# A bank table of eight rows for the attention groups in which VectorE raises two scores

## Chip, cores and metric

The kernel runs on one core of one Trainium2 chip. The metric is the device time of one execution in microseconds (us). TensorE is called PE, VectorE DVE, ScalarE ACT and GpSimd POOL, as the profile calls them.

## The reference

One token matrix x of 2048 rows and 512 columns goes through two branches, and a gate per row mixes them:

```
x = A_x
g = _sigmoid((x * gate_w).sum(-1, keepdims=True))
a = _A_ref(x, A_wqkv, A_wo)        # softmax attention: 32 heads of 16, no mask, then wo
b = _B_ref(x, B_w1, B_b1, B_w2, B_b2)   # layer norm, MLP over the token axis, gelu
return g * a + (1 - g) * b
```

In the attention, `scores = q k^T / 4`, `p = softmax(scores)` and `o = p v`, all in fp32.

## The kernel before, in words

The kernel first projects q, k and v, then runs the first layer of the MLP. After that comes the attention stage, which fills the last three quarters of the time and into which the MLP's second layer and the output projection are woven. Only this stage is touched.

**Groups and phases.** There are 32 groups; a group is a pair of heads and one half (1024) of the query columns. A group has eight phases. In each phase PE computes eight score tiles of 128 keys by 512 queries (line 922). Each is a *unit*, numbered 0 to 7 in the order of its score within the phase. A score uses 64 rows of PE's array, and a matmul of the woven-in work (line 1045) runs on the other 64 rows beside most of them, six or eight per phase. Then PE applies the exponentials of the *phase before* to v (`apply_v`, line 878), called *the AV block* here: two instructions per unit, each of them two passes, so 32 passes for eight units, into one bank that holds the sums of the block. DVE adds that bank to the group's running sum (line 898), in one piece or two.

**Who takes the exponentials.** ACT does, in five instructions per phase: two units alone, then three pairs of units whose banks are neighbours (line 945). In 21 of the groups, `EXTRA` (0 to 10 and 15 to 24), the two units of one pair in phase 2 (`EXTRA_PH`) go to DVE instead: `steps_of_exp` reads both banks out (line 985, here called *the two raises*), and nine further DVE instructions per unit, spread over the phases behind, compute the power of two. The raises are issued behind the last score of the phase. To level the AV blocks, a pair of phase 1 is held back from the block of phase 2 and goes into that of phase 3, and the raised pair joins the block after phase 7. The blocks in phases 1 to 7 so have 32, 24, 32, 32, 32, 32 and 32 passes, and the one in phase 0 has 40 when it follows a group of `EXTRA`.

**Banks.** Of the eight PSUM banks, seven are a ring for scores and AV sums (`RING`, the tile `s`), and one holds the woven-in work (`dn`). Which bank each score of a phase gets, which units ACT takes together and in which order, and which bank the AV block writes, is a row of the table `TURN`, used in turn by phase number modulo 3. A score waits until the last reader of its bank has finished: the exponential of the unit that was there, or DVE's addition if it held AV sums. The AV block waits likewise for the reader of its own bank. In all three rows of `TURN` that bank held unit 1 of the same phase, which ACT reads as its second exponential.

**Order.** The stage is written under a manual schedule: every engine executes its instructions in the order of the program text, and the waits between engines come from the recorded reads and writes (`reads`, `writes`). DVE's other work (`slow`, the split of weights, the nine steps) is dealt out phase by phase, ahead of the phase's scores in the text. At a phase's end the text has the raises (in phase 2 of the 21 groups), the AV block and DVE's addition.

Of the kernel before, what the change touches and what calls it, by code (L numbers as in the profile page):

```python
# [76 lines left out]
def gated_mix(ctx: ExitStack, tc: tile.TileContext, a_x, a_wqkv, a_wo, b_w1, b_b1, b_w2, b_b2, gate_w, out):  # L77
# [28 lines left out]
    g = const.tile([P, NS], F32, name="g")  # L106
# [23 lines left out]
    order = {f0: [(c + (NS // 2 if f0 + NB >= F else 0)) % NS for c in range(NS)] for f0 in range(0, F, NB)}  # L130
# [58 lines left out]
    with tc.tile_pool(name="vp", bufs=1, side="right") as pool:  # L189
# [165 lines left out]
        e = pool.tile([P, NS], F32, name="e")  # L355
# [115 lines left out]
    with tc.tile_pool(name="ln1", bufs=3, side="right") as ln, tc.tile_pool(name="gl", bufs=2, side="right") as gl:  # L471
# [21 lines left out]
        beside = {mybir.EngineType.Activation, mybir.EngineType.DVE, mybir.EngineType.Pool}  # L493
# [6 lines left out]
        for f0, cs in order.items():  # L500
            n = min(NB, F - f0) // P
# [68 lines left out]
    for step in gelus:  # L570
# [10 lines left out]


    TURN = [
# [3 lines left out]
    ]  # L587
# [157 lines left out]
    N_S = 8  # L745
# [34 lines left out]
    done, at = at, put_outputs(range(NH), 6, 12, at)  # L780
    at = put_outputs(range(NH, NS), 0, EARLY, at)
# [41 lines left out]
    EXTRA = *range(0, 11), *range(15, 25)  # L823
    EXTRA_PH = 2
# [38 lines left out]
    def apply_v(late, bank):  # L863

        if not late:
            return
        g, units = late
        pairs = list(zip(*([u for u in units if u[2] == qb] for qb in range(2))))
        assert 2 * len(pairs) == len(units)
        av = banks[:, bank, :]  # L870
        taken = [0, 0]

        for pair in pairs:
            for i, c, qb, pt, act in pair:
                taken[qb] += 1
                for h in range(2):
                    j = 2 * qb + h
                    mm = nc.tensor.matmul(  # L878
                        av[32 * j : 32 * j + VC, i * QC : (i + 1) * QC],
                        v[:, c, g % NP * 2 + i, :],  # L880
                        pt[:, h * QC : (h + 1) * QC],
                        start=taken[qb] == 1,
                        stop=taken[qb] == len(pairs),
                    )
                    writes(mm, bank, j, act)

        there = {(i, qb) for i, _, qb, *_ in units}
        if len(there) == 4:
            parts = [(sums[g], av)]
        else:  # L890
            parts = []
            for i in sorted(range(2), key=lambda i: -sum(k[0] == i for k in there)):
                qbs = [qb for qb in range(2) if (i, qb) in there]
                if qbs:
                    at = slice(64 * qbs[0], 64 * (qbs[-1] + 1)), slice(i * QC, (i + 1) * QC)
                    parts.append((sums[g][at], av[at]))
        for x, y in parts:
            reads(nc.vector.tensor_tensor(x, y, x, ALU.add), bank)  # L898

    engines = {getattr(mybir.EngineType, name) for name in ("PE", "Activation", "DVE", "Pool", "SP")}  # L900
    with tc.manual_schedule(engines=engines):
        kt, qt = {0: k_bufs[0]}, {0: q_bufs[0]}
        late, fence = None, None
# [8 lines left out]
                next(step)  # L912
        full(first)

        pt = None

        def score(grp, i, n, turn, exps, units, apart):
# [4 lines left out]
            mm = nc.tensor.matmul(  # L922
                banks[:, bank, :],
                kt[grp][rows, c * P : (c + 1) * P],
                qt[grp][rows, qb * NB : (qb + 1) * NB],
                start=True,
                stop=True,
            )
            writes(mm, bank)
            units.append([i, c, qb, None, None])  # L930
            for which in exps:
                if which[-1] == len(units) - 1:
                    if which == apart:
                        steps_of_exp(turn, units, which)
                    else:
                        exponential(turn, units, which)

        def exponential(turn, units, which):
            nonlocal pt
            if which[0] != 1:  # L940
                pt = ptp.tile([P, 2, NB], F32, name="pt")
            which = sorted(which, key=lambda m: turn[m])
            first, at = which == [1], [turn[m] for m in which]
            dst = pt[:, first : first + len(at), :]
            act = nc.scalar.activation(dst, banks[:, at[0] : at[-1] + 1, :], AF.Exp, scale=SCALE)  # L945
            reads(act, *at)
            for n, m in enumerate(which):
                units[m][3:] = dst[:, n, :], act

        def steps_of_exp(turn, units, which):  # L950

# [36 lines left out]
                reads(ins, turn[m])  # L988
                exp_steps.extend(steps(n, units[m]))

        def without(units, which):
            return [units[m] for m in which], [u for m, u in enumerate(units) if m not in which]

        exp_steps, held, apart = [], [], []
        for grp in range(NG):
            at = [0, 0]
            for ph in range(2 * TWOS):
# [7 lines left out]
                two, second = divmod(ph, 2)  # L1005
# [5 lines left out]
                if not second:  # L1011
                    for what, *args in calls.get(two, ()):
                        what(*args)
                    beside = [step(*args) for step, *args in dense.get(two, ())]
# [16 lines left out]
                    room -= cost  # L1031
                    step()
                units = []
                turn, exps, av_bank = TURN[(2 * two + second) % len(TURN)]

                qbs = [0, 1, 0, 1, 0, 1, *((1, 0) if len(beside) == 6 else (0, 1))]
                pair = [e for e in exps if len(e) == 2 and qbs[e[0]] != qbs[e[1]]][-1]
                alone = pair if grp in EXTRA and ph == EXTRA_PH else None
                half = slice(0, HALF) if second else slice(HALF, P)
                for m, (ps, a, b, first, last, done) in enumerate(beside):  # L1040
                    score(grp, second, at[second], turn, exps, units, alone)
                    if grp == ph == 0 and m < 4:
                        next(gelus[m % 2])
                    at[second] += 1
                    mm = nc.tensor.matmul(ps, a[half], b[half], start=first and not second, stop=last and bool(second))  # L1045
                    if m == 0 and fence is not None:
                        tc.add_manual_dep(mm.ins, fence.ins.name, SYNC, reason=REASON)
                    if m == len(beside) - 1:
                        fence = nc.gpsimd.memset(token, 0.0)  # L1049
                        tc.add_manual_dep(fence.ins, mm.ins.name, SYNC, reason=REASON)  # L1050
                    if done and second:
                        done()
                for n in range(N_S - len(beside)):
                    i = (n + second + 1) % 2
                    score(grp, i, at[i], turn, exps, units, alone)
                    at[i] += 1
                if splits:
                    split_weight(nc.vector.tensor_copy)
# [15 lines left out]
                late = grp, units  # L1074
        assert not slow and not soon and not exp_steps


# [12 lines left out]
            nc.scalar.copy(hi[i], whole[i])  # L1090

        divided(0)
        apply_v(late, TURN[(2 * two + second + 1) % len(TURN)][-1])
# [138 lines left out]
```

## Time and profile before

| | |
|---|---|
| median of 3 runs | 1271.02 us (1270.91 to 1281.69) |
| the profiled execution | 1272.05 us; from its first to its last instruction 1270.3 us |
| granted PE clock in it | 0.998 |
| PE busy, its weight loads | 99%, 63% of the span |
| ACT, DVE, POOL busy | 84%, 57%, 18% |
| exponentials on ACT (line 945) | 1259 instructions, 943.6 us |
| scores, AV passes | 2048 and 8024 + 168 |
| first score, last AV pass | 295.8 us, 1252.8 us from the span's start |

Matmuls are pipelined and drawn longer than the distance between them, so PE reads as busy nearly always. Its waits show in the start times of its instructions and as idle time of its weight loads (PEld), which wait in its place. ACT's instructions are drawn long too when one queues behind another.

### The profile page before, as it was taken

The numbers are of one execution on the slowest core, as the hardware profiler recorded it, in microseconds if no ns is written. First come the engines' busy times: TensorE is split into PE (matmuls) and PEld (weight loads), VectorE is DVE, ScalarE is ACT, GpSimd is POOL, SyncE is SP. The second block draws the span as 40 slices with busy tenths as digits, with TensorE's granted clock in tenths as the row PEclk, the third lists the DMA queues.
The fourth block names the chain that finished last, engine by engine and source line by source line (L and its number), as shares of the span: only waits on it lengthen the run. The fifth ranks groups of instructions, "written<-read, shape, count | busy, mean of one in ns | idle before, by whom it ended". The sixth has DMA issues, their size and how long they took to land.

```text
span 1270.3 us, 33073 instructions
## 1 busy us (share of the span) xinstructions
PE 1262.1 (99%) x13230; PEld 796.6 (63%) x13230; DVE 721.5 (57%) x1326; ACT 1072.3 (84%) x1484; POOL 228.7 (18%) x447
## 2 busy tenths in 40 slices
PE   9999999999999999999999999999999999999998
PEld 7888888886555555555555555555555555555555
DVE  6775361536776776666634346676666662325425
ACT  4444343438999999999999999999999999999994
POOL 4510244553111111111110011111111111100000
PEclk9999999999999999999999999999999999999999
DMA  6787644326343443334555533333433345547621
GB/s 189 217 294 296 225 134 130 95 75 134 72 93 60 77 86 69 77 66 82 121 102 132 117 64 71 68 73 76 74 75 70 76 87 105 99 87 204 142 62 70
DMA packets 101826, 141.19 MB, mean 111 GB/s; under 512 B 17161, under 2 KB 62495, under 8 KB 98528
## 3 DMA queue, kind: packets, MB, share of 16 engines
q1 hardware_dynamic: 101232, 138.20, 46.2%
q8 instruction: 106, 1.74, 0.7%
q10 hardware_dynamic: 432, 0.79, 0.2%
q14 instruction: 56, 0.46, 0.1%
HBM read 102.77 MB, written 36.16 MB: 109 GB/s over the span
## 4 chain that ended last, share of the span: by engine, by line
PE 98%; DMA 0%; DVE 0%; ACT 0%; SPq 0%; issue 0%; ACTq 0%
PE s L878 38%; PE s L922 35%; PE acc L469 12%; PE acc L91 10%; PE dn L1045 2%; PE pa L1116 1%; DMA x<-in_A_x_dram 0%; PE acc L299 0%; PE pa L1125 0%; PE dn L908 0%; PE acc L210 0%; DVE ot L482 0%; SPq L202 0%; DVE base L1144 0%; DVE row L482 0%; ACT row L484 0%
## 5 line engine op out<-in xcount | busy, mean ns | idle before, releaser
L945 ACT ACTIVATE pt<-s 128x512 f32<-128x512 f32 (+1 forms) x1259 | 943.6, 962 | 10.3 <-PE s L922 4.4
L922 PE MATMUL s<-qs,ks 64*128 64x512 f32 x2048 | 493.9, 404 | 0.1
L878 PE MATMUL s<-pt,v 128*17 128x256 f32 x8024 | 482.6, 381 | 0.0
L922 PEld LDWEIGHTS s<-qs,ks 64*128 64x128 f32 x2048 | 325.4, 184 | 170.3 <-ACT pt L945 90.9
L898 DVE TENSOR_TENSOR ot<-s,ot 128x256 f32<-128x256 f32 (+2 forms) x427 | 190.5, 448 | 352.9 <-PE s L878 275.9
L878 PEld LDWEIGHTS s<-pt,v 128*17 128x17 f32 x8024 | 210.3, 97 | 231.9 <-ACT pt L945 82.9
L1045 PE MATMUL dn<-u_hi,w_hi 64*128 64x512 f32 x428 | 186.4, 436 | 0.0
L84 POOL TENSOR_TENSOR w_lo<-w_raw,w_hi 128x512 fp32r<-128x512 f32 (+1 forms) x127 | 150.7, 1189 | 167.9 <-ACT w_hi L83 105.1
L1045 PE MATMUL dn<-u_lo,w_hi 64*128 64x512 f32 x430 | 170.0, 395 | 0.0
L1045 PE MATMUL dn<-u_hi,w_lo 64*128 64x512 f32 x430 | 169.1, 393 | 0.0
L1049 POOL MEMSET token<- 1x1 f32 x256 | 26.2, 102 | 782.6 <-PE dn L1045 704.4
L967 DVE SCALAR_TENSOR_TENSOR row<-row,o_hi 128x512 f32<-128x512 f32 x168 | 116.6, 694 | 4.9
L83 ACT CAST w_hi<-w_raw 128x512 fp32r<-128x512 f32 (+1 forms) x67 | 37.8, 568 | 76.6 <-PE acc L469 57.1
L469 PE MATMUL acc<-h_hi,w_lo 128*128 128x512 f32 x224 | 87.2, 389 | 0.0
L469 PE MATMUL acc<-h_hi,w_hi 128*128 128x512 f32 x224 | 87.1, 389 | 0.0
L469 PE MATMUL acc<-h_lo,w_hi 128*128 128x512 f32 x224 | 87.1, 389 | 0.0
L1045 PEld LDWEIGHTS dn<-u_hi,w_lo 64*128 64x128 f32 x430 | 79.3, 184 | 0.9
L1045 PEld LDWEIGHTS dn<-u_lo,w_hi 64*128 64x128 f32 x430 | 79.4, 185 | 0.3
L1045 PEld LDWEIGHTS dn<-u_hi,w_hi 64*128 64x128 f32 x428 | 78.6, 184 | 0.7
L91 PE MATMUL acc<-xt_hi,wc_hi 128*128 128x512 f32 x128 | 49.8, 389 | 0.0
L91 PE MATMUL acc<-xt_lo,wc_hi 128*128 128x512 f32 x128 | 49.8, 389 | 0.0
L91 PE MATMUL acc<-xt_hi,wc_lo 128*128 128x512 f32 x128 | 49.8, 389 | 0.0
(160 smaller groups left out, 1156.6 us busy)
## 6 DMA issues: line engine op xcount, KB each, us to landing
w_raw<-in_B_w_dram SPq DMA_DIRECT2D x96, 256.0 KB
ks<-kp SPq DMA_DIRECT2D x192, 128.0 KB
qs<-qp SPq DMA_DIRECT2D x256, 64.0 KB
qp<-pc SPq DMA_DIRECT2D x16, 768.0 KB
x<-in_A_x_dram SPq DMA_DIRECT2D x32, 256.0 KB
kp<-pc SPq DMA_DIRECT2D x16, 512.0 KB
w_raw<-in_B_w_dram SPq DMA_DIRECT2D x32, 128.0 KB
bp<-row SPq DMA_DIRECT2D x16, 256.0 KB
```

The source lines that it names most:

```text
L83: copy(hi, src)
L84: return sub(lo, src, hi.bitcast(F32), ALU.subtract)
L91: nc.tensor.matmul(ps, a, b, start=start and n == 0, stop=stop and n == last)
L469: nc.tensor.matmul(p, a, b, start=first and k == 0, stop=last and k == 2)
L878: mm = nc.tensor.matmul(av[32 * j : 32 * j + VC, i * QC : (i + 1) * QC], v[:, c, g % NP * 2 + i, :], pt[:, h * QC : (h + 1) * QC], start=t ...
L898: reads(nc.vector.tensor_tensor(x, y, x, ALU.add), bank)
L922: mm = nc.tensor.matmul(banks[:, bank, :], kt[grp][rows, c * P : (c + 1) * P], qt[grp][rows, qb * NB : (qb + 1) * NB], start=True, stop=True,)
L945: act = nc.scalar.activation(dst, banks[:, at[0] : at[-1] + 1, :], AF.Exp, scale=SCALE)
L967: nc.vector.scalar_tensor_tensor(box[1], q or box[1], a, x, ALU.add, ALU.mult)
L1045: mm = nc.tensor.matmul(ps, a[half], b[half], start=first and not second, stop=last and bool(second))
L1049: fence = nc.gpsimd.memset(token, 0.0)
L1116: nc.tensor.matmul(pa[t], a, b, start=i == 0 and t not in LATE, stop=i == len(mms) - 1 and t in LATE)
```

## The change

A second table, `LEAN`, is used in the 21 groups of `EXTRA`: eight rows, one for each phase of a group. `TURN` goes on serving the other eleven groups. Each row of either table gets a fourth entry that says in which order the AV block later takes the units: `None` keeps the order of the scores, `True` takes pairs of neighbouring scores in the order in which their exponentials end, and `False` pairs them anew in the order of the exponentials. The raised units are no longer the last fitting pair of the row but units 1 and 7 (`APART`) of phase 2, taken out of that row's exponentials. Exponentials now leave a queue in the row's order, each when its last score has been issued. The AV pairs are matched when a phase ends (`matched`), and held or set aside as pairs; the number of passes per block stays.

```diff
     TURN = [
-        ((3, 4, 5, 6, 0, 1, 2, 3), ((0,), (1,), (2, 3), (4, 5), (6, 7)), 4),
+        ((3, 4, 5, 6, 0, 1, 2, 3), ((0,), (1,), (2, 3), (4, 5), (6, 7)), 4, None),
...
+    LEAN = [
+        ((4, 1, 0, 3, 6, 5, 2, 4), ((0,), (2,), (5, 4), (1, 6), (3, 7)), 0, False),
...
+        ((1, 4, 0, 3, 6, 5, 2, 1), ((0,), (7, 2), (4,), (5, 1), (3, 6)), 4, True),
...
+        ((3, 1, 2, 4, 0, 5, 3, 6), ((0,), (2,), (4, 1), (7, 5), (3, 6)), 2, True),
...
+        ((3, 2, 1, 4, 0, 6, 5, 3), ((0,), (1,), (4, 2), (3, 7), (6, 5)), 2, False),
+    ]
+    APART = (1, 7)
...
             units.append([i, c, qb, None, None])
-            for which in exps:
-                if which[-1] == len(units) - 1:
-                    if which == apart:
-                        steps_of_exp(turn, units, which)
-                    else:
-                        exponential(turn, units, which)
+            if apart and len(units) - 1 == apart[-1]:
+                steps_of_exp(turn, units, apart)
+            while queue and max(queue[0]) < len(units):
+                exponential(turn, units, queue.pop(0))
...
-                turn, exps, av_bank = TURN[(2 * two + second) % len(TURN)]
-
-                qbs = [0, 1, 0, 1, 0, 1, *((1, 0) if len(beside) == 6 else (0, 1))]
-                pair = [e for e in exps if len(e) == 2 and qbs[e[0]] != qbs[e[1]]][-1]
-                alone = pair if grp in EXTRA and ph == EXTRA_PH else None
+                table = LEAN[ph] if grp in EXTRA else TURN[(2 * two + second) % len(TURN)]
+                turn, exps, av_bank, by_end = table
+                apart = APART if grp in EXTRA and ph == EXTRA_PH else ()
+                exps = [e for e in ([m for m in e if m not in apart] for e in exps) if e]
+                queue, spare = list(exps), None
...
+                assert not queue
+                pairs = matched(units, exps, False if apart else by_end)
                 if grp in EXTRA:
 
                     if ph == EXTRA_PH - 1:
-                        held, units = without(units, pair)
+                        held = [pairs.pop()]
                     elif ph == EXTRA_PH:
-                        apart, units = without(units, pair)
-                        units = held + units
+                        away = [tuple(sorted((units[m] for m in apart), key=lambda u: u[2]))]
+                        pairs = held + pairs
                     elif ph == 2 * TWOS - 1:
-                        units = units + apart
-                late = grp, units
+                        pairs = pairs + away
+                late = grp, pairs
```

The rows of `LEAN` shown are those of phases 0, 2, 5 and 7. The first bracket of a row has the banks of the eight scores, the second the exponentials, the number behind them is the AV block's bank. The rows of phases 1, 3, 4 and 6 begin `(6, 5, 2, 4, ...)`, `(6, 0, 2, 1, ...)`, `(1, 0, 4, 3, ...)` and `(5, 0, 6, 1, 2, ...)`; their AV banks are 2, 2, 0 and 0.

**How instructions move: PE, phase 2 of the fifth group of `EXTRA`.** `s` is the ring, `qs` and `ks` are the stacked q and k, `dn` is the woven-in work; behind a row stands the engine whose semaphore it waits for. The rows from the last beside-matmul to the AV block, before:

```order
L1045 MATMUL dn<-u_hi,w_lo 128x512
L922 MATMUL s<-qs_2748,ks_2750 128x512 [waits DVE_49]
L922 MATMUL s<-qs_2748,ks_2750 128x512 [waits Activation_49]
L878 MATMUL s<-pt,v 17x256 [waits Activation_49]
L878 MATMUL s<-pt,v 17x256 x11
```

and now:

```order
L1064 MATMUL dn<-u_hi,w_lo 128x512
L932 MATMUL s<-qs_2748,ks_2750 128x512 [waits DVE_49]
L932 MATMUL s<-qs_2748,ks_2750 128x512 [waits Activation_49]
L888 MATMUL s<-pt,v 17x256 [waits DVE_49]
L888 MATMUL s<-pt,v 17x256 x11
```

The AV block's first instruction waits for DVE in place of ACT: its bank 4 now held unit 1, and DVE reads that. It is so in all 21 groups, and was in none before.

**DVE, the same phase, as it stands now** (the third group; before, the rows are the same with lines 898 and 985, and the last has no wait):

```order
L84 TENSOR_TENSOR wo_lo<-o_sum,wo_hi 128x512 [waits DVE_49]
L1007 TENSOR_SCALAR o_hi<-s 128x512 [waits PE_49]
L1007 TENSOR_SCALAR o_hi<-s 128x512 [waits Activation_49]
L908 TENSOR_TENSOR ot<-s,ot 128x256 [waits PE_49,Activation_49]
L908 TENSOR_TENSOR ot<-s,ot 64x256 [waits Activation_49]
```

The two raises stay where they were. The first has a wait for PE, the second has none for PE; in two groups (the second and third) a weight split of two instructions stands right ahead of them, in the other 19 DVE's addition does.

**PE, phase 5 of the fifth group.** Before, scores 2 to 6 and what they wait for:

```order
L922 MATMUL s<-qs_2748,ks_2750 128x512 [waits Activation_49]
L1045 MATMUL dn<-u_hi,w_lo 128x512
L922 MATMUL s<-qs_2748,ks_2750 128x512
L1045 MATMUL dn<-u_hi,w_hi 128x512
L922 MATMUL s<-qs_2748,ks_2750 128x512 [waits Activation_49]
L1045 MATMUL dn<-u_lo,w_hi 128x512
L922 MATMUL s<-qs_2748,ks_2750 128x512
L1045 MATMUL dn<-u_hi,w_lo 128x512
L922 MATMUL s<-qs_2748,ks_2750 128x512 [waits DVE_49]
```

The same scores now:

```order
L932 MATMUL s<-qs_2748,ks_2750 128x512
L1064 MATMUL dn<-u_hi,w_lo 128x512
L932 MATMUL s<-qs_2748,ks_2750 128x512
L1064 MATMUL dn<-u_hi,w_hi 128x512
L932 MATMUL s<-qs_2748,ks_2750 128x512 [waits DVE_49]
L1064 MATMUL dn<-u_lo,w_hi 128x512
L932 MATMUL s<-qs_2748,ks_2750 128x512 [waits Activation_49]
L1064 MATMUL dn<-u_hi,w_lo 128x512
L932 MATMUL s<-qs_2748,ks_2750 128x512 [waits Activation_49]
```

The bank of the last AV block, which DVE's addition must free, is written again by score 4 and no longer by score 6. So it is in phases 5, 6 and 7; in phases 3 and 4 it is score 5, in phases 0 to 2 score 6 as before.

More of the change, by code (lines that the diff above doesn't have):

```diff
@@ L866, in apply_v @@
             return
-        g, units = late
-        pairs = list(zip(*([u for u in units if u[2] == qb] for qb in range(2))))
-        assert 2 * len(pairs) == len(units)
+        g, pairs = late
+        assert all([u[2] for u in pair] == [0, 1] for pair in pairs)
         av = banks[:, bank, :]
@@ L885, in apply_v @@
                     writes(mm, bank, j, act)
-        there = {(i, qb) for i, _, qb, *_ in units}
+        there = {(i, qb) for pair in pairs for i, _, qb, *_ in pair}
         if len(there) == 4:
@@ L913, in gated_mix, with score @@
         full(first)
-        pt = None
-        def score(grp, i, n, turn, exps, units, apart):
+        spare = None
+        def score(grp, i, n, turn, queue, units, apart):
             c, qb = n // 2, (n + i) % 2
@@ L948, in exponential, with matched @@
                 units[m][3:] = dst[:, n, :], act
+        def matched(units, exps, by_end):
+            order = [m for e in exps for m in e]
+            if by_end is False:
+                return list(zip(*([units[m] for m in order if units[m][2] == qb] for qb in range(2))))
+            pairs = [sorted((m, m + 1), key=lambda m: units[m][2]) for m in range(0, N_S, 2)]
+            if by_end:
+                pairs.sort(key=lambda pair: max(order.index(m) for m in pair))
+            return [tuple(units[m] for m in pair) for pair in pairs]
         def steps_of_exp(turn, units, which):
@@ L989, in steps_of_exp @@
                 exp_steps.extend(steps(n, units[m]))
-        def without(units, which):
-            return [units[m] for m in which], [u for m, u in enumerate(units) if m not in which]
-        exp_steps, held, apart = [], [], []
+        exp_steps, held, away = [], [], []
         for grp in range(NG):
@@ L1033, in gated_mix @@
                 units = []
-                turn, exps, av_bank = TURN[(2 * two + second) % len(TURN)]
-                qbs = [0, 1, 0, 1, 0, 1, *((1, 0) if len(beside) == 6 else (0, 1))]
-                pair = [e for e in exps if len(e) == 2 and qbs[e[0]] != qbs[e[1]]][-1]
-                alone = pair if grp in EXTRA and ph == EXTRA_PH else None
+                table = LEAN[ph] if grp in EXTRA else TURN[(2 * two + second) % len(TURN)]
[3 more added lines that the diff above has]
+                queue, spare = list(exps), None
                 half = slice(0, HALF) if second else slice(HALF, P)
                 for m, (ps, a, b, first, last, done) in enumerate(beside):
-                    score(grp, second, at[second], turn, exps, units, alone)
+                    score(grp, second, at[second], turn, queue, units, apart)
                     if grp == ph == 0 and m < 4:
@@ L1054, in gated_mix @@
                     i = (n + second + 1) % 2
-                    score(grp, i, at[i], turn, exps, units, alone)
+                    score(grp, i, at[i], turn, queue, units, apart)
                     at[i] += 1
@@ L1092, in gated_mix @@
         divided(0)
-        apply_v(late, TURN[(2 * two + second + 1) % len(TURN)][-1])
+        apply_v(late, TURN[(2 * two + second + 1) % len(TURN)][2])
         divided(1)
```

15 lines of the change are left out of this document (10 added, 5 removed), and 8 rows, old and new, of tables (LEAN, TURN).

## Prediction

> **What bounds the kernel now.** I read the page first, its chain of waits above all, then the attention stage phase by phase.
>
> ```profile
> PE 98%; DMA 0%; DVE 0%; ACT 0%; SPq 0%; issue 0%; ACTq 0%
> ...
> L922 PEld LDWEIGHTS s<-qs,ks 64*128 64x128 f32 x2048 | 325.4, 184 | 170.3 <-ACT pt L945 90.9
> ...
> L878 PEld LDWEIGHTS s<-pt,v 128*17 128x17 f32 x8024 | 210.3, 97 | 231.9 <-ACT pt L945 82.9
> ```
>
> The chain is PE's nearly throughout, so a wait put into PE's queue moves the end. PE's own waits in the stage are put down to ACT. How much of that is real shows in the phases of group 18, one of the 21, cut at the first score of each (phase 0 to 7):
>
> ```profile
> 831.17:835.33 4.16, 4.16 (x58) 2.38 (x55) 2.68 (x5) 4.16 (x6) 1.84 (x3) 1.00 0.61 170
> 835.33:838.99 3.66, 3.66 (x50) 2.08 (x47) 1.03 (x2) 3.54 (x6) 1.38 (x2) 1.00 0.50 130
> 838.99:842.23 3.24, 3.24 (x42) 1.84 (x39) 2.13 (x4) 3.24 (x5) 0.09 (x1) 1.00 0.74 135
> 842.23:845.90 3.66, 3.66 (x50) 2.10 (x47) 2.84 (x6) 3.40 (x6) 0.09 (x1) 1.00 0.99 113
> 845.90:849.57 3.67, 3.67 (x50) 2.08 (x47) 3.02 (x5) 3.67 (x6) 0.09 (x1) 1.00 0.47 64
> 849.57:853.25 3.68, 3.68 (x50) 2.12 (x47) 2.87 (x6) 3.68 (x6) 0.48 (x2) 1.00 0.01 2
> 853.25:856.96 3.71, 3.71 (x50) 2.14 (x47) 2.93 (x5) 3.71 (x6) 0.43 (x2) 1.00 0.03 7
> 856.96:860.68 3.73, 3.73 (x50) 2.14 (x47) 3.27 (x6) 3.73 (x6) 0.62 (x2) 1.00 0.15 35
> ```
>
> Behind the window stands its length in us. An undisturbed phase with a block of 32 passes takes 3.66. The block of phase 2 has 24 passes and saves 0.42, so phase 0, with 40, would take some 4.08 undisturbed. Phases 5, 6, 7 and 0 are longer than that by 0.02, 0.05, 0.07 and 0.08: that is all that waiting costs here, 0.22 us a group. Its cause is seen in a group whose exponentials are all ACT's:
>
> ```profile
> 720.35:724.08 3.73, 3.73 (x50) 2.14 (x47) 0.85 (x2) 3.73 (x6) 0.09 (x1) 1.00 0.99 146
> ```
>
> There ACT sets the pace at 3.73. In a group of the 21 it falls 0.07 behind in each 3.66 phase after the relief of phase 2, until the AV block, whose bank ACT's second exponential reads, waits for it. If all of this went, 21 x 0.22 = 4.6 us would be won, 0.4% of the time: the ceiling of any gain here.
>
> **The wait added in phase 2.** The AV block's bank there is now unit 1's, and its reader is the first raise on DVE. What that means is in the same phase of group 18, PE first, then DVE:
>
> ```profile
> 838.99 0.50 PE L922 MATMUL s<-qs,ks 64*128 64x512 f32 x1
> ...
> 839.33 0.39 PE L922 MATMUL s<-qs,ks 64*128 64x512 f32 x1
> ...
> 840.49 0.40 PE L922 MATMUL s<-qs,ks 64*128 64x512 f32 x2
> 840.81 1.49 PE L878 MATMUL s<-pt,v 128*17 128x256 f32 x24
> 842.23 0.50 PE L922 MATMUL s<-qs,ks 64*128 64x512 f32 x1
> ```
>
> ```profile
> 839.28 0.88 DVE L898 TENSOR_TENSOR ot<-s,ot 128x256 f32<-128x256 f32 x2 [2.72 <-DMA o<-ot]
> 840.96 1.29 DVE L985 TENSOR_SCALAR o_hi<-s 128x512 f32<-128x512 f32 x2 [0.79 <-PE s L922]
> ```
>
> ```profile
> L985 DVE TENSOR_SCALAR o_hi<-s x42: 679/686/693, 307.0 to 1019.0; 128x512 f32<-128x512 f32 x42
> ...
>   PE s L922: 15.0, 19
> ```
>
> DVE has added by 840.16 and idles 0.79 for PE. This group uses the third row of `TURN`, so the raised units are 3 and 7; unit 3 was scored three scores before the last, and still the first raise begins 0.47 behind the last two scores (840.49). In the order of the program the first raise has a wait for PE and the second has none for PE: one wait, on the last score, serves both. Nothing of that is changed, so with units 1 and 7 the first raise begins at 840.96 again and takes 0.69. What PE needs to notice it is seen where a late addition held up a score:
>
> ```profile
> 1016.92 0.88 DVE L898 TENSOR_TENSOR ot<-s,ot 128x256 f32<-128x256 f32 x2 [3.43 <-DMA s<-ot]
> ...
> 1017.86 0.19 PEld L922 LDWEIGHTS s<-qs,ks 64*128 64x128 f32 x2 [0.35 <-DVE ot L898]
> ```
>
> The addition ends at 1017.80, the score's weight load starts at 1017.86: 0.06. So the block starts at 840.96 + 0.69 + 0.06 = 841.71 where it started at 840.81, **0.90 us later**. Behind it in PE's queue stands the next phase; nothing of PE's can run meanwhile. Times 21: **18.9 us**. In two groups a weight split stands ahead of the raises on DVE:
>
> ```profile
> 336.20 0.69 DVE L84 TENSOR_TENSOR wo_lo<-o_sum,wo_hi 128x512 fp32r<-128x512 f32 x1
> 336.92 1.29 DVE L985 TENSOR_SCALAR o_hi<-s 128x512 f32<-128x512 f32 x2
> ```
>
> ```profile
> 336.42 1.49 PE L878 MATMUL s<-pt,v 128*17 128x256 f32 x24
> ```
>
> There the block starts at 336.92 + 0.75 = 337.67 where it was 336.42, 1.25 later: 2 x 0.35 = **0.7 us** more. So far that cost nothing, since the block's bank was ACT's. Phase 2 also has four exponentials alone and one pair, one instruction more on ACT; even a whole exponential of 0.60 lies inside PE's new pause of 0.9:
>
> ```profile
> 842.77 0.60 ACT L945 ACTIVATE pt<-s 128x512 f32<-128x512 f32 x1 [0.26 <-PE s L922]
> ```
>
> **The addition that must be done sooner.** In phases 5 to 7 score 4 takes the bank that DVE's addition frees. Phase 5 of group 18, DVE and PE:
>
> ```profile
> 849.78 0.88 DVE L898 TENSOR_TENSOR ot<-s,ot 128x256 f32<-128x256 f32 x2 [0.59 <-PE s L878]
> ```
>
> ```profile
> 849.57 0.50 PE L922 MATMUL s<-qs,ks 64*128 64x512 f32 x1
> ...
> 850.61 0.39 PE L922 MATMUL s<-qs,ks 64*128 64x512 f32 x1
> ```
>
> The addition ends at 850.66, noticed at 850.72; score 4 stood at 850.61. It loses 0.11, and the phase takes 3.77: +0.09 in phase 5, +0.04 in phase 7. In phase 6 the addition's two pieces follow each other closer (no wait between them in the program's order) and are just in time. If phase 6 loses 0.11 too, that is 2.3 us more in all. Before, the bank was due two scores later, and nothing waited for it.
>
> **What goes.** With 0.90 us more in phase 2 and 0.11 in phases 5 and 7 ACT catches up, and its lag no longer reaches the AV block: -0.08 in phase 0, -0.05 in phase 6. Per group beside the 0.90: 0.09 + 0.04 - 0.08 - 0.05 = 0.00. The two halves cancel.
>
> **Where the tables meet** (groups 10 to 11, 14 to 15, 24 to 25) one table's early scores fall on banks that the other frees late. The last pair of a phase and the next phase's first score:
>
> ```profile
> 860.26 1.27 ACT L945 ACTIVATE pt<-s 128x1024 f32<-128x1024 f32 x1
> ```
>
> ```profile
> 860.68 0.50 PE L922 MATMUL s<-qs,ks 64*128 64x512 f32 x1
> ```
>
> The pair ends at 861.53, 0.85 into the phase, noticed at 0.91. Group 11's first score wants bank 5, read by the last pair of group 10: +0.9 at most, 0.8 with ACT less late. Group 15's second score, due 0.34 into the phase (839.33 against 838.99), wants bank 1, read by the last pair: +0.5. Group 25's second score wants bank 2, the AV bank, free at 1.09 + 0.06: +0.8. Together **2.1 us**, once.
>
> **Sum:** 18.9 + 0.7 + 0.0 + 2.1 = 21.7 us. The profiled execution took 1272.05 (span 1270.3 and 1.75 around it), so it would take 1293.8; against the median of 1271.02 it is **1292.7 us**, 1.7% slower.
>
> **Rivals.**
>
> *The first raise is not late.* Place: its wait for PE. If it ended with unit 1's score (the second of the phase), DVE would be free at 840.16, begin 0.03 later (as from 336.89 to 336.92 above), the raise be done at 840.88, the block at 840.94: 0.13 instead of 0.90. The point from which it decides: a first raise that starts before 840.06 costs nothing. Then 21 x 0.13 + 2 x 1.1 (the weight split still stands ahead) + 2.1 = 7 us: 1278, 0.6% more and not to be told from no change. For it speaks only that unit 1 is scored early; against it the 0.79 of idling with unit 3 and the single wait. 5%, since what decides it is in the trace.
>
> *The block waits for both raises.* Then it starts at 840.96 + 1.29 + 0.06 = 842.31, 1.50 later: 21 x 1.50 + 2.8 = 34 us, 1305. For it: both raises write one tile. Against it: the second raise reads unit 7's bank, which is not the block's. 3%.
>
> *The clock falls.* PE now stands still for 0.8 us 21 times, more than in any window above, all of which were granted 1.00. If each pause cost one phase at half the clock, 3.66 more, it would be 21 x 3.66 = 77 on top: 1370. No window shows a fall, and the pause is a quarter of a phase: 2%. The Trainium skill bears on this (TensorE: Matmul & The Clock Gate, "A second HAM failure mode: psum-queue depth-cycling"): frequent short idling between groups of matmuls can make the clock swing between half and full. The same page ("What's actually happening") puts the fall behind an idle window of about 3.4 us, which the pause does not fill. The windows above, all at 1.00, hold no pause that long, so no run has shown it yet.
>
> **How the numbers follow.** The forecast has 90%. Its own spread: the raise differs by 0.01, the noticing by perhaps 0.05, the cancelling halves by 0.15 a group, that is 21 x 0.2 = 4 us either way, and the meetings by up to 1. So 1287 to 1298 holds it, and with it more than 8 in 10; the rivals lie outside. A measurement of this kernel can tell 1% from no change, 12.7 us: the forecast, the double wait and the clock are slower by more (95% less 2% for a forecast missed far), the early raise is within it (5% and 1%), and a gain above 1% exceeds the 4.6 us ceiling (1%).
>
> **What would show it.** Right: phase 2 of the 21 groups at 4.1 us, its AV block released by the raise on DVE with about 0.9 us of PE idling; phases 5 and 7 at 3.77 with score 4 released by the addition; phases 0 and 6 at 4.08 and 3.66; the other eleven groups as before but for the three meetings. Wrong: a first raise that starts before the last score; a phase 2 near 3.3; a clock under 0.99; phases 3 to 7 that sum to more than 18.6.

## The result and the profile after

| | before | changed |
|---|---|---|
| time, median | 1271.03 us (6 runs) | 1302.92 us (6 runs, 1302.51 to 1303.61) |
| ratio | | 1.0239, 95% interval 1.021 to 1.0268 |
| span of the profiled execution | 1270.3 us | 1300.8 us |
| mean granted clock | 0.998 | 0.999 |

The medians differ by 31.9 us, 2.5%, inside the interval of the ratio; one of the six runs of the kernel before took 1281.69 us, the others 1270.6 to 1271.93. The forecast was 21.7 us, and the measured time lies above the stated range. In the page of the changed kernel, first the chain of waits, then two rows of the groups (busy time and mean, then the idle time ahead of them):

```profile
PE 90%; ACT 5%; issue 2%; DVE 2%; DMA 0%; SPq 0%; ACTq 0%; DVEq 0%
...
L888 PE MATMUL s<-pt,v 128*17 128x256 f32 x8024 | 482.6, 381 | 17.9 <-DVE o_hi L1007 17.9
L932 PEld LDWEIGHTS s<-qs,ks 64*128 64x128 f32 x2048 | 315.2, 184 | 187.3 <-ACT pt L958 102.2
```

The chain is no longer PE's alone, and the AV matmuls have got an idle time of 17.9 us whose releaser is the raise. That one row gives the size of the wait in phase 2, and it leaves 14 of the 31.9 us unexplained. Group 18 again, cut at the first score of its phases; phases 0, 2, 5, 6 and 7:

```profile
851.82:855.91 4.09, 4.09 (x58) 2.31 (x55) 2.58 (x5) 4.04 (x6) 2.05 (x3) 1.00 0.76 172
...
859.58:863.68 4.10, 3.30 (x42) 1.85 (x39) 2.14 (x4) 3.58 (x6) 0.09 (x1) 1.00 0.83 136
...
871.04:874.93 3.89, 3.89 (x50) 2.00 (x47) 2.87 (x6) 3.88 (x6) 0.91 (x2) 1.00 0.00 0
874.93:879.17 4.24, 3.93 (x50) 2.01 (x47) 2.93 (x5) 3.83 (x6) 0.21 (x2) 1.00 0.02 6
879.17:883.06 3.89, 3.89 (x50) 2.00 (x46) 3.40 (x6) 3.83 (x6) 0.62 (x2) 1.00 0.12 32
```

Phase 2 has grown from 3.24 to 4.10, and PE is busy for only 3.30 of it. Phases 5 and 7 have grown from 3.68 and 3.73 to 3.89, though PE counts as busy throughout: what is lost there does not show as idle time. Phase 6 of this group is longer than in the others (in the median group it takes 3.87), because its addition starts 0.58 into the phase in place of 0.21; why it does in this one group was not found. The clock was 1.00 in all of them.

The next table sums, over the 21 groups, the changed kernel's phases less those of the kernel before, in us; a phase runs from its first score to the next phase's first. The experiments told below stand in it in the same way, and the last column sums the stage from its first score to the start of its last phase:

| kernel | ph 0 | 1 | 2 | 3 | 4 | 5 | 6 | 7 | other groups | all |
|---|---|---|---|---|---|---|---|---|---|---|
| the change | -0.5 | 0.5 | 18.7 | -0.2 | 0.1 | 4.5 | 3.9 | 4.1 | 0.9 | 31.9 |
| early raise | -0.4 | 0.6 | 4.2 | -0.2 | 0.1 | 4.9 | 3.5 | 4.1 | 1.0 | 17.7 |
| units 5 and 7 | -0.6 | 0.4 | -0.7 | 0.1 | 0.1 | 4.5 | 3.9 | 4.1 | 0.9 | 12.7 |
| one piece | 0.6 | 0.4 | 18.8 | -0.2 | 0.0 | 0.0 | 0.0 | 0.8 | 1.0 | 21.4 |
| score 3 | -0.5 | 0.5 | 18.7 | -0.2 | 0.1 | 9.5 | 8.8 | 8.7 | 1.1 | 46.6 |
| units 5 and 7, one piece | 0.6 | 0.6 | -0.6 | 0.0 | 0.1 | 0.1 | -0.1 | 0.7 | 0.9 | 2.3 |
| units 5 and 7, score 5 | 0.9 | 0.4 | -0.7 | 0.0 | 0.0 | 1.5 | 1.3 | 1.3 | 0.9 | 5.8 |
| same partitions | -0.5 | 0.7 | 18.7 | -0.2 | 0.0 | 4.5 | 1.5 | 4.1 | 1.0 | 29.7 |

The loss sits in two places: phase 2, which was forecast, and phases 5 to 7, where 1.7 us were forecast and 12.4 came (0.75 of that is the first meeting of the tables, in phase 7 of group 10). The 31.9 of the last column equals the difference of the medians; the two profiled spans differ by 30.5, since in that execution of the changed kernel the stretches ahead of the first score and from the last phase on were together 1.3 shorter.

**Phase 2** of group 18, PE's rows and then DVE's, with the idle time ahead of a row and its releaser in brackets:

```profile
860.84 0.61 PE L932 MATMUL s<-qs,ks 64*128 64x512 f32 x3
862.26 1.49 PE L888 MATMUL s<-pt,v 128*17 128x256 f32 x24 [0.81 <-DVE o_hi L1007]
863.68 0.50 PE L932 MATMUL s<-qs,ks 64*128 64x512 f32 x1
```

```profile
859.87 0.88 DVE L908 TENSOR_TENSOR ot<-s,ot 128x256 f32<-128x256 f32 x2 [2.72 <-ACT pt L958]
861.51 1.29 DVE L1007 TENSOR_SCALAR o_hi<-s 128x512 f32<-128x512 f32 x2 [0.77 <-PE s L932]
```

DVE idles 0.77 until the last score, the first raise runs from 861.51 to 862.20, and the AV block follows at 862.26. The second raise is still running then (to 862.80): the block waits for the first alone.

**Phase 5** of group 18: PE, PE's weight loads, DVE.

```profile
871.38 0.39 PE L932 MATMUL s<-qs,ks 64*128 64x512 f32 x1
...
871.61 0.39 PE L932 MATMUL s<-qs,ks 64*128 64x512 f32 x1
...
871.84 0.39 PE L932 MATMUL s<-qs,ks 64*128 64x512 f32 x1
...
872.18 0.49 PE L932 MATMUL s<-qs,ks 64*128 64x512 f32 x1
...
872.52 0.39 PE L932 MATMUL s<-qs,ks 64*128 64x512 f32 x1
...
872.75 0.40 PE L932 MATMUL s<-qs,ks 64*128 64x512 f32 x2
```

```profile
871.38 0.18 PEld L932 LDWEIGHTS s<-qs,ks 64*128 64x128 f32 x1
...
871.62 0.18 PEld L932 LDWEIGHTS s<-qs,ks 64*128 64x128 f32 x1
...
872.18 0.18 PEld L932 LDWEIGHTS s<-qs,ks 64*128 64x128 f32 x1 [0.38 <-DVE ot L908]
...
872.29 0.19 PEld L932 LDWEIGHTS s<-qs,ks 64*128 64x128 f32 x1
```

```profile
871.25 0.88 DVE L908 TENSOR_TENSOR ot<-s,ot 128x256 f32<-128x256 f32 x2 [0.61 <-PE s L888]
```

And score 5 in the same phase of the kernel before, which starts at 849.57:

```profile
850.84 0.39 PE L922 MATMUL s<-qs,ks 64*128 64x512 f32 x1
```

In an undisturbed stretch the weight load of a score runs one step, 0.23, ahead of its own matmul: the loads at 871.38 and 871.62 belong to the matmuls at 871.61 and 871.84. The Trainium skill has it so (TensorE: Matmul & The Clock Gate, "Step-by-step: what each phase is for"): weight loads are pulled ahead of the matmuls in flight. These rows agree. Score 4's load would have started at 871.84, but it carries the wait for the addition (done at 872.13) and starts at 872.18, 0.34 late. Its matmul starts with it instead of behind it, is drawn 0.49 long in place of 0.39, and the next score follows 0.34 later (872.52) in place of 0.23. So score 5 stands 1.48 into the phase, where it stood at 1.27: the phase loses 0.21 and not 0.11. PE counts as busy throughout because its matmuls are drawn 0.39 to 0.49 long, longer than even the step of 0.34.

**Phase 6**, in group 5 since group 18's is unusual (it starts at 475.11): DVE, then PE.

```profile
475.32 0.86 DVE L908 TENSOR_TENSOR ot<-s,ot 128x256 f32<-128x256 f32 x2 [0.64 <-PE s L888]
```

```profile
475.92 0.39 PE L932 MATMUL s<-qs,ks 64*128 64x512 f32 x1
...
476.24 0.50 PE L932 MATMUL s<-qs,ks 64*128 64x512 f32 x1
...
476.58 0.39 PE L932 MATMUL s<-qs,ks 64*128 64x512 f32 x1
```

The two pieces take 0.86 together, against 0.88 with a wait between them: having no wait in the order has won 0.02. Score 4 is held here as well, to 1.13 into the phase.

### The profile page after: what moved, and what is told of

Its sections match the earlier page's. It is cut to its first block, busy times and chain, and to the rows that moved or that the text cites. A ratio compares the mean times of both kernels' runs of the same rounds, so it can differ in the third digit from the quotient of the medians.

```text
span 1300.8 us, 33107 instructions
## 1 busy us (share of the span) xinstructions
PE 1273.3 (98%) x13230; PEld 786.5 (60%) x13230; DVE 728.1 (56%) x1333; ACT 1082.8 (83%) x1505; POOL 230.3 (18%) x447
## 4 chain that ended last, share of the span: by engine, by line
PE 90%; ACT 5%; issue 2%; DVE 2%; DMA 0%; SPq 0%; ACTq 0%; DVEq 0%
PE s L888 33%; PE s L932 32%; PE acc L469 12%; PE acc L91 10%; ACT pt L958 5%; PE dn L1064 2%; DVE o_hi L1007 1%; PE pa L1137 1%; PE acc L299 0%; DMA x<-in_A_x_dram 0%; DVE ot L908 0%; PE pa L1146 0%; PE dn L918 0%; PE acc L210 0%; DVE ot L482 0%
## 5 line engine op out<-in xcount | busy, mean ns | idle before, releaser
L958 ACT ACTIVATE pt<-s 128x1024 f32<-128x1024 f32 (+1 forms) x1280 | 953.8, 893 | 31.8 <-PE s L932 25.6
L932 PE MATMUL s<-qs,ks 64*128 64x512 f32 x2048 | 506.7, 407 | 2.2 <-ACT pt L958 1.1
L888 PE MATMUL s<-pt,v 128*17 128x256 f32 x8024 | 482.6, 381 | 17.9 <-DVE o_hi L1007 17.9
L932 PEld LDWEIGHTS s<-qs,ks 64*128 64x128 f32 x2048 | 315.2, 184 | 187.3 <-ACT pt L958 102.2
L908 DVE TENSOR_TENSOR ot<-s,ot 128x256 f32<-128x256 f32 (+1 forms) x434 | 196.0, 452 | 376.7 <-PE s L888 287.4
L1064 PE MATMUL dn<-u_lo,w_hi 64*128 64x512 f32 x430 | 176.3, 410 | 0.0
```

What stands on the lines that cost most here:

```text
L888: mm = nc.tensor.matmul(av[32 * j : 32 * j + VC, i * QC : (i + 1) * QC], v[:, c, g % NP * 2 + i, :], pt[:, h * QC : (h + 1) * QC], start=t ...
L932: mm = nc.tensor.matmul(banks[:, bank, :], kt[grp][rows, c * P : (c + 1) * P], qt[grp][rows, qb * NB : (qb + 1) * NB], start=True, stop=True,)
```

## The experiments

The theory after the result: the change costs two separate things, the AV block's wait in phase 2 and a held score in each of phases 5, 6 and 7, and a held score costs its wait and about 0.10 more. The kernel before, timed again beside the experiments, took 1270.88 us (7 runs) and 1271.05 us (14 runs), so times are compared across them. The rivals: phase 2 loses by the order of its banks or by both raises; phases 5 to 7 pay for something else in the new rows; the price of a hold grows with its length.

**Early raise.** The raise of unit 1 is issued behind its own score, the raise of unit 7 behind the last.

```diff
-            if apart and len(units) - 1 == apart[-1]:
-                steps_of_exp(turn, units, apart)
+            if len(units) - 1 in apart:
+                steps_of_exp(turn, units, len(units) - 1)
...
```

> The whole computation is done. The raise of unit 1 is written right behind unit 1's own score, so that its wait for PE no longer covers the last score; unit 7's stays behind the last score. Theory (the first raise is late because of that one wait): in group 18 the addition is done 1.17 into phase 2 (859.87 + 0.88 - 859.58), so the raise runs from 1.20 to 1.89 and the AV block starts at 1.95 instead of 2.68: phase 2 falls from 4.13 to about 3.40, 21 x 0.73 = 15.3 us, and the two groups with a weight split ahead of the raises give 0.4 each more: 1302.9 - 16 = 1287, 1286 to 1289. Rival (the block waits until both raises have read, or DVE's reading of a bank holds PE's writing to its neighbours): the block still starts at about 2.6 and the time stays within 2 us of 1303.

Measured: 1288.53 us (4 runs), 14.4 less than the change and 1.0140 of the kernel before (1.0123 to 1.0157). Phase 2 of group 5 (it starts at 457.73), DVE, then PE:

```profile
458.02 0.88 DVE L908 TENSOR_TENSOR ot<-s,ot 128x256 f32<-128x256 f32 x2 [2.74 <-ACT pt L958]
458.94 1.45 DVE L1019 TENSOR_SCALAR o_hi<-s 128x512 f32<-128x512 f32 x2
```

```profile
459.23 0.40 PE L932 MATMUL s<-qs,ks 64*128 64x512 f32 x2
459.69 1.49 PE L888 MATMUL s<-pt,v 128*17 128x256 f32 x24
461.11 0.50 PE L932 MATMUL s<-qs,ks 64*128 64x512 f32 x1
```

The raise starts right behind the addition, no longer behind the last score, and the block starts at 1.95 into the phase as expected (median of the 21 groups; it was 2.71), with the second raise still ahead. The lateness of the first raise was its one wait for PE on the last score. This is the prediction's rival of a raise that is not late, made true, and the 0.13 that it put on what is left in phase 2 (1.95 against 1.82) is met. One item of the expectation missed: the two groups with a weight split gain nothing (1.25 and 1.33 over the kernel before, as in the change), so they hold 2.6 of the 4.2 us that phase 2 still loses. The prediction's rival had them so, with the split still ahead of the raise.

**Units 5 and 7.** ACT takes unit 1 and with it the AV block's bank again.

```diff
-        ((1, 4, 0, 3, 6, 5, 2, 1), ((0,), (7, 2), (4,), (5, 1), (3, 6)), 4, True),
+        ((1, 4, 0, 3, 6, 5, 2, 1), ((0,), (1,), (2,), (4,), (3, 6)), 4, True),
...
-    APART = (1, 7)
+    APART = (5, 7)
```

> The whole computation is done. DVE raises units 5 and 7 instead of 1 and 7 in phase 2, and ACT takes unit 1 as its second exponential, so that the bank of the AV block is read by ACT, as it was before the change. Everything else of the new table stays. Theory (the whole of phase 2's loss is the wait of the AV block for the raise of the unit that shares its bank): phase 2 returns from 4.13 to about 3.24, that is 21 x 0.88 = 18.5 us, some 0.9 more from the groups with a weight split, and up to 2 back where ACT's lag reaches PE again: 1302.9 - 18.5 = 1284.4, 1283 to 1287. Rival (the table's order of banks in phase 2 is what costs, whoever reads them): phase 2 stays above 3.8 and the time above 1295.

Measured: 1283.40 us (4 runs), 19.5 less than the change, 1.0100 of the kernel before (1.0083 to 1.0117). Phase 2 of group 18, from 846.64:

```profile
846.64:849.87 3.23, 3.23 (x42) 1.85 (x39) 2.14 (x4) 3.23 (x6) 0.09 (x1) 1.00 0.78 146
```

The order of the banks in phase 2 stayed. Units 1 and 5 changed readers, so that ACT reads the AV block's bank again, as its second exponential, and the whole loss of the phase is gone, here and in the sum over the groups (18.7 to -0.7). Phases 5 to 7 lose as before.

**One piece.**

```diff
...
-        for x, y in parts:
+        for x, y in parts[: 1 if short else 2]:
...
-                apply_v(late, av_bank)
+                apply_v(late, av_bank, grp in EXTRA and ph in (4, 5, 6))
```

> Left out: in the 21 groups, the second of the two pieces of DVE's addition behind the AV blocks of phases 4, 5 and 6 (the sums of those blocks are incomplete). The addition in phases 5, 6 and 7 is then done at 0.63 into the phase instead of 1.07 to 1.09, before score 4 is due at 1.03, so that no score is held. Theory A (a held score costs its wait of 0.11 and then about 0.10 more, since PE's stream starts again without weights loaded ahead): phases 5 to 7 fall from 3.89, 3.87 and 3.89 to 3.67 to 3.73, 0.15 to 0.22 each, 21 x (0.5 to 0.6) = 10 to 13 us: 1290 to 1293. Theory B (the hold costs the 0.11 of the wait alone, and the rest of the 10 us that these phases lost has another cause, such as the order of the banks or ACT's exponentials): 21 x (0.11 + 0.10 + 0.11) = 7 us at most and phases 5 to 7 stay near 3.78: 1296 to 1299.

Measured: 1292.18 us (4 runs), 10.7 less than the change, 1.0168 of the kernel before (1.0151 to 1.0185). Phases 5, 6 and 7 of group 18:

```profile
864.24:867.92 3.68, 3.68 (x50) 2.07 (x47) 2.35 (x5) 3.68 (x6) 0.82 (x2) 1.00 0.00 0
867.92:871.62 3.70, 3.70 (x50) 2.20 (x47) 2.41 (x4) 3.70 (x6) 0.09 (x1) 1.00 0.02 4
871.62:875.36 3.74, 3.74 (x52) 2.21 (x48) 2.74 (x5) 3.74 (x6) 0.85 (x2) 1.00 0.11 37
```

They are back at the 3.68, 3.71 and 3.73 of the kernel before, ACT's growing lag included. The held score is what these phases lost, and it cost about 0.2 each, not 0.11. This run also spares DVE the second piece, 0.44 us a phase; the runs with score 3 and score 5 below keep that work. Phase 0 takes 1.1 us more than in the change: with no pause left in phases 5 to 7 ACT's lag reaches the AV block there again.

**Score 3.** Scores 3 and 4 change banks in phases 5 to 7.

```diff
-        ((3, 1, 2, 4, 0, 5, 3, 6), ((0,), (2,), (4, 1), (7, 5), (3, 6)), 2, True),
-        ((5, 0, 6, 1, 2, 4, 3, 5), ((0,), (1,), (3, 4), (5, 6), (2, 7)), 0, False),
-        ((3, 2, 1, 4, 0, 6, 5, 3), ((0,), (1,), (4, 2), (3, 7), (6, 5)), 2, False),
+        ((3, 1, 2, 0, 4, 5, 3, 6), ((0,), (2,), (3, 1), (7, 5), (4, 6)), 2, True),
+        ((5, 0, 6, 2, 1, 4, 3, 5), ((0,), (1,), (3, 4), (5, 6), (2, 7)), 0, False),
+        ((3, 2, 1, 0, 4, 6, 5, 3), ((0,), (1,), (3, 2), (4, 7), (6, 5)), 2, False),
```

> The whole computation is done. In the rows of phases 5, 6 and 7 scores 3 and 4 change banks, so that score 3, due at 0.80, wants the bank that the addition frees at 1.14, instead of score 4 (due at 1.03). The wait grows from 0.11 to 0.34. Theory A (a wait and a fixed price of about 0.10 for starting again, whatever the wait): each of the three phases grows by the 0.23 alone, 3.89 to 4.12, 63 x 0.23 = 14.5 us: 1317, 1314 to 1320. Theory B (the price grows with the wait, which the phase pays about twice): each grows by 0.45, 63 x 0.45 = 28 us: 1331. Theory C (no price of starting again; what the phases lost is not the hold): the phases pay 0.34 in place of what they lost, 0.22, 63 x 0.12 = 8 us: 1311.

Measured: 1317.40 us (4 runs), 14.5 more than the change, 1.0368 of the kernel before (1.0351 to 1.0386). Phases 5, 6 and 7 of group 5, and the loads of the first of them:

```profile
474.55:478.68 4.13, 3.94 (x50) 2.01 (x47) 3.12 (x6) 4.13 (x6) 0.68 (x2) 1.00 0.03 11
478.68:482.78 4.10, 3.94 (x50) 2.00 (x47) 2.93 (x5) 3.71 (x6) 0.79 (x2) 1.00 0.40 121
482.78:486.91 4.13, 3.94 (x50) 2.00 (x47) 3.26 (x6) 4.06 (x6) 0.53 (x2) 1.00 0.09 26
```

```profile
474.89 0.18 PEld L932 LDWEIGHTS s<-qs,ks 64*128 64x128 f32 x1
...
475.69 0.18 PEld L932 LDWEIGHTS s<-qs,ks 64*128 64x128 f32 x1 [0.62 <-DVE ot L908]
```

The wait grew by a step of 0.23, and so did each phase (3.89, 3.87, 3.89 to 4.13, 4.10, 4.13). The price beside the wait does not grow with it: theory A, to the microsecond; the other two were 14 and 6 us off.

**Units 5 and 7, and one piece,** both edits together:

> Left out: as in the run with one piece, the second piece of DVE's addition behind the AV blocks of phases 4, 5 and 6 of the 21 groups. DVE raises units 5 and 7, as in the run of that name. Theory (the wait in phase 2 and the held scores of phases 5 to 7 are two separate losses, and with the meetings of the tables they are all that the change costs): the gains of the two runs add, 1302.9 - 19.5 - 10.7 = 1272.7, which is also the time of the kernel before plus the 2.4 us of the three meetings: 1272 to 1275. Rival (the two overlap: one of them hides part of the other, or frees ACT time that the other needs): the gains do not add, and the time stays above 1277.

Measured: 1273.10 us (10 runs), 1.0017 of the kernel before (1.0007 to 1.0026). In the sums of the phases the two gains over the change were 31.9 - 12.7 = 19.2 and 31.9 - 21.4 = 10.5, together 29.7; both edits gain 29.6. What is left, 2.3 us, is about the size of the meetings (2.5).

**Units 5 and 7, and score 5.** The edit of units 5 and 7 stays; beside it phases 5 to 7 give the freed bank to score 5, and the third exponential then takes unit 5 in place of unit 4.

```diff
-        ((3, 1, 2, 4, 0, 5, 3, 6), ((0,), (2,), (4, 1), (7, 5), (3, 6)), 2, True),
-        ((5, 0, 6, 1, 2, 4, 3, 5), ((0,), (1,), (3, 4), (5, 6), (2, 7)), 0, False),
-        ((3, 2, 1, 4, 0, 6, 5, 3), ((0,), (1,), (4, 2), (3, 7), (6, 5)), 2, False),
+        ((3, 1, 2, 4, 5, 0, 3, 6), ((0,), (2,), (5, 1), (7, 4), (3, 6)), 2, True),
+        ((5, 0, 6, 1, 4, 2, 3, 5), ((0,), (1,), (3, 5), (4, 6), (2, 7)), 0, False),
+        ((3, 2, 1, 4, 6, 0, 5, 3), ((0,), (1,), (5, 2), (3, 7), (6, 4)), 2, False),
...
```

> The whole computation is done. Units 5 and 7 are raised, and in phases 5, 6 and 7 the bank that the addition frees goes to score 5, due at 1.26 into the phase, in place of score 4, due at 1.03; the addition is done at 1.07 to 1.09. The rest of the new table stays. Theory (a score is held only if its bank comes free behind its turn, and with no hold there is no starting again): phases 5 to 7 at 3.67 to 3.75, the time of before plus 2.4 us of meetings and up to 2 of ACT's lag: 1273 to 1276. Rival (the addition is noticed later than 1.15, or another bank of these rows comes free too late): phases 5 to 7 stay above 3.80 and the time above 1279.

Measured: 1276.20 us (5 runs), 1.0040 of the kernel before (1.0026 to 1.0054), 0.2 above the upper end of what was expected. Phases 5 to 7 of group 5, and in the first of them the addition, the load that waits for it and the matmul of that load:

```profile
463.83:467.58 3.76, 3.75 (x50) 2.06 (x47) 3.12 (x6) 3.74 (x6) 0.31 (x2) 1.00 0.00 0
467.58:471.36 3.78, 3.78 (x46) 2.30 (x47) 2.93 (x5) 3.78 (x6) 1.16 (x2) 1.00 0.46 143
471.36:475.12 3.76, 3.76 (x50) 2.17 (x47) 3.27 (x6) 3.76 (x6) 0.19 (x2) 1.00 0.17 35
```

```profile
464.03 0.88 DVE L908 TENSOR_TENSOR ot<-s,ot 128x256 f32<-128x256 f32 x2 [0.58 <-PE s L888]
```

```profile
464.97 0.18 PEld L932 LDWEIGHTS s<-qs,ks 64*128 64x128 f32 x1
```

```profile
465.10 0.39 PE L932 MATMUL s<-qs,ks 64*128 64x512 f32 x1
```

The addition ends at 464.91, and the load of score 5 starts 0.11 late (464.97; one step ahead of its matmul would be 464.86), and the matmul stands where it always stood, 1.27 into the phase: this hold cost nothing. The phases still take 0.06 to 0.07 more than before in the mean of the 21 groups. A possible reason is that ACT, busy nearly throughout all three, sets the pace, since its third exponential now needs score 5. That reading was not tried by itself.

**Same partitions.** The prediction took the two pieces of phase 6 to follow each other closely. They do not; what holds the second?

```diff
...
+                    if low and qbs == [1]:
+                        qbs = [0]
                     at = slice(64 * qbs[0], 64 * (qbs[-1] + 1)), slice(i * QC, (i + 1) * QC)
...
-                apply_v(late, av_bank)
+                apply_v(late, av_bank, grp in EXTRA and ph == 5)
```

> Changed: in the 21 groups the second piece of the addition that runs in phase 6 takes partitions 0 to 63 in place of 64 to 127 (that part of the sums is therefore not the sum that is wanted). Its size and its place in DVE's queue stay, and it has no wait of its own. Theory (the second piece starts only when the first has ended because it begins at another partition; pieces that begin at the same partition overlap, as a step behind a piece that begins at partition 0 did at 0.55 into the phase in the run with one piece): the pieces run from 0.21 to 0.63 and from 0.55 to 0.98, score 4 is not held in phase 6 (due 1.03) and phase 6 falls from 3.87 to 3.68 to 3.73: 21 x 0.16 = 3.4 us, 1299.5, 1298 to 1301. Rival (the second piece waits for the first for another reason, such as both reading one bank): the pieces stay one behind the other, phase 6 at 3.87 and the time at 1303.

Measured: 1300.62 us (4 runs), 2.3 less than the change, 1.0232 of the kernel before (1.0216 to 1.0249). Phase 6 of group 5, DVE, then PE's loads, then its matmuls:

```profile
474.71 0.75 DVE L910 TENSOR_TENSOR ot<-s,ot 128x256 f32<-128x256 f32 x2 [0.65 <-PE s L888]
475.39 0.67 DVE L988 SCALAR_TENSOR_TENSOR o_hi<-row,o_hi 128x512 f32<-128x512 f32 x1
```

```profile
475.08 0.18 PEld L934 LDWEIGHTS s<-qs,ks 64*128 64x128 f32 x1
...
475.52 0.18 PEld L934 LDWEIGHTS s<-qs,ks 64*128 64x128 f32 x1 [0.25 <-DVE ot L910]
```

```profile
475.31 0.39 PE L934 MATMUL s<-qs,ks 64*128 64x512 f32 x1
...
475.54 0.47 PE L934 MATMUL s<-qs,ks 64*128 64x512 f32 x1
...
475.85 0.39 PE L934 MATMUL s<-qs,ks 64*128 64x512 f32 x1
```

With both pieces from partition 0 they overlap and take 0.75 in place of 0.86: here the second waits for the first only when it begins elsewhere. The Trainium skill says so (VectorE: DVE Perf Modes, "Two Vector instructions with no wait between them"): an instruction whose operands begin in another group of 32 partitions than those ahead of it starts only when the earlier ones have finished. Both halves agree here, 0.86 from partition 64 and 0.75 from partition 0. The gain was smaller than the expected 3.4: score 4's matmul is on time (475.54), but its load came 0.21 late (475.52 for 475.31), and the next score follows 0.31 later in place of 0.23. So a load can be late, cost 0.08, and no matmul ever be seen to wait.

**The holds in one row each.** Over the 21 groups, medians: how late the load of the score that waits for the addition starts, and how late the score behind it stands.

| kernel, phase | load late | next score late |
|---|---|---|
| score 5, phase 5 | 0.11 | 0.00 |
| same partitions, phase 6 | 0.21 | 0.08 |
| the change, phase 6 | 0.32 | 0.20 |
| the change, phases 5 and 7 | 0.34 | 0.215 |
| score 3, phase 6 | 0.555 | 0.43 |
| score 3, phases 5 and 7 | 0.574 | 0.446 |

In all six the loss is the lateness of the load less 0.12 to 0.13, and nothing when that is below zero. The rows say why: undisturbed, from a load to the matmul behind its own are two steps, 0.465; from a held load they are 0.335 (872.18 to 872.52). The difference is the slack. Theory A's "wait and 0.10" is the same line wherever the matmul waits too (0.34 less 0.13 is 0.11 and 0.10); the same-partitions row is where they part, 0.08 against nothing. The line was drawn through these runs, and no further run tried it; group 18's odd phase 6, whose load came 0.69 late and cost 0.57, was not used for it and lies on it.

## Why the prediction was wrong in size

The direction, the main mechanism and its price held. By its own steps, in us (forecast, then measured; the phases' sums are those of the table above):

| step | forecast | measured |
|---|---|---|
| AV block of phase 2, with the two weight splits | 18.9 + 0.7 | 18.7 |
| phases 5, 6 and 7, without the meeting | 1.7 | 11.7 |
| ACT's lag gone from phase 0, with phase 1 | -1.7 | -0.8 |
| three meetings of the tables | 2.1 | 2.5 |
| the rest | 0 | -0.1 |
| sum | 21.7 | 31.9 (the terms are rounded) |

*The wait in phase 2: right.* The block moved from 1.82 to 2.71 into the phase (medians), the releaser is the raise, and the first raise is late for the reason given. It came a little below the forecast since in three groups phase 2 grew by only 0.7 (it had already lost 0.2 there before, to a late addition), and the two groups with a weight split grew by 1.25 and 1.33 as forecast. Units 5 and 7 and the early raise show it from both sides. The rival of a block that waits for both raises named 1305, near the measured time, but for a wrong reason: the block starts while the second raise runs.

*"It loses 0.11, and the phase takes 3.77": the step that failed.* It set the addition's end and notice against the start of score 4's matmul. What waits for the bank is the score's weight load, and that runs one step ahead; against the load the addition is 0.34 late, and 0.13 of that is slack, which leaves 0.21. One of the rows that the prediction itself quotes, the load at 1017.86 that it used for the 0.06, is a load that a late addition released; it was used for the delay of the notice alone. The mechanism, a score held by the addition, was named; its size was half the true one. In two phases that is 21 x 0.2 = 4.2 us.

*"In phase 6 the two pieces are just in time": also failed,* 21 x 0.2 = 4.2 us more. The absence of a wait in the program's order was read as overlap, but the second piece begins at partition 64 and is held by DVE itself. The alternative named there, a phase 6 that loses 0.11 too, priced at 2.3, was on the right side and again half of it. These two steps are 8.4 of the 10.0 us by which phases 5 to 7 were missed. Group 18's odd phase 6 is 0.4 more, and the rest, some 0.02 a phase, stays open.

*"The two cancelling halves": failed with them.* ACT's lag did go, but phases 5 to 7, with that lag gone, lost 0.55 a group, against the 0.08 that follows from the forecast (0.09 + 0.04 - 0.05). The range allowed 0.15 a group for these halves; they came out 0.47 above.

*Meetings, clock: right.* 2.5 against 2.1 for the meetings. No window of the changed kernel is under 1.00: with the 21 pauses of 0.8 the granted clock over the stage (296 to 1250) is 1.00, and its mean over the execution is 0.999.

Of the listed signs, "phases 3 to 7 that sum to more than 18.6" is the one that came true (medians: 3.68 + 3.67 + 3.89 + 3.87 + 3.89 = 19.0). Of the signs of being right, phase 6 at 3.66 and phases 5 and 7 at 3.77 did not come.

## What to carry to other kernels

Where a PSUM bank comes free just before a matmul needs it, set the release against that matmul's weight load and not against the matmul: in this stream the load stands 0.23 us earlier, and only some 0.13 of its lateness is forgiven. Such a loss hides in a PE row that is busy from end to end; it shows in the step from one matmul to the next and in the releaser in the PEld rows. And when a bank changes its reader, ask of the new reader when it starts, not how long it takes: of the 0.87 lost in phase 2, all but 0.13 was one wait that covered the last score.

## What was not expected of the hardware

- A load held for 0.11 us cost nothing; at 0.21 it cost 0.08 though no matmul was seen to wait; from there to 0.57, the longest median hold here, every further 0.1 of lateness cost 0.1.
- After a load held for 0.32 or more the matmul starts together with its load, is drawn 0.49 in place of 0.39, and the next score follows after 0.335 in place of 0.23.
- The two pieces of the addition, without a wait between them, took 0.86 us with the second from partition 64 and 0.75 with both from partition 0; with a wait they took 0.88.
